# Attention and two feed-forward layers on one core: TensorE's order written out from pair seven on, with transposes as two 64-row products

## The chip, the core and the metric

The kernel runs on one core of one Trainium2 chip. The metric is the device time of one execution in microseconds, the median of three runs. The core's engines are TensorE (PE in the profile, its weight loads PEld), VectorE (DVE), ScalarE (ACT), GpSimd (POOL) and SyncE (SP), which issues nearly all DMAs.

## The reference

There are 4 batches of 8 heads, 576 positions and a head size of 64. The attention's output, as 2304 tokens of 512 features, goes through two feed-forward layers, of inner size 1536 and 2048.

```
    scores = scale * np.matmul(q, k.transpose(0, 1, 3, 2))
    log_f = np.log(np.clip(f, 0.0001, 1.0))
    cum = np.cumsum(log_f, axis=-1)
    decay = cum[:, :, :, None] - cum[:, :, None, :]
    ...
    scores = np.where(causal, -1000000000.0, scores + decay)
    scores = scores - np.max(scores, axis=-1, keepdims=True)
    attn = np.exp(scores)
    attn = attn / (np.sum(attn, axis=-1, keepdims=True) + 1e-09)
    return np.matmul(attn, v).astype(np.float32)
...
    gate = 1.0 / (1.0 + np.exp(-(x @ w_gate)))
    val = x @ w_val
    return (gate * val @ w_out).astype(np.float32)
...
    h = x @ w_in
    relu6 = np.clip(h + 3.0, 0.0, 6.0)
    g = h * relu6 / 6.0
    return (g @ w_out).astype(np.float32)
```

## The kernel before, in words

**Attention** works on 16 pairs of heads, four per batch. A pair has four units, which are blocks of 128 query rows (s = 1, 2, 3, of which s = 1 holds the first two blocks) and the tail of 64 rows of both heads (s = 4). Pairs 0 to 6 take them upwards, pairs 7 to 15 downwards (4, 3, 2, 1). One unit passes through these stages:

- `scores`: products `st<-kp,qp`, one per head, each on 64 of the array's rows, or `st<-kp,qz` on all 128 rows for the tail. Each writes its own one of three PSUM banks (`psA`).
- `expo`: VectorE adds the decay and takes the row minimum (L443), ScalarE exponentiates (L451). `norm`: VectorE takes the reciprocal (L485, L486), GpSimd multiplies (L488).
- `flip`: TensorE transposes the 128x128 blocks of `e` with an identity into `tt` or `t5` (three banks, `psB`), ScalarE copies them to `etA` (s = 1) or `etB` (L525). A pair has 25 such blocks: 5, 8, 6 and 6 for s = 4, 3, 2, 1. `etA` and `etB` exist once each, so a pair's first copy into `etB` waits until the pair before has read it.
- `values`: `pv<-etB,vn` and `pv<-etA,vn`, on 64 columns of the array for each head. ScalarE and VectorE split the result into two parts (`x`, L550, L551), and `store` sends them to DRAM (`x_d`, L555).

The loop over t does `scores` of unit t, `norm` of t - 1, `flip` of t - 2 and `values` of the pair whose last unit was t - 3.

**Feed-forward groups as filler.** While attention runs, TensorE also works on the first layer for chunks of 512 tokens, in groups of 12 products of 128x512: `pg<-big,wg` (gate), `pv<-big,wv` (value), `po<-big,wo` (down). A group's four feature blocks are read back from `x_d` into `big` (L205), one block for each head pair of a batch, so the last block of a chunk is there only after the batch's last pair is stored. Chunk 1 needs pair 7, chunk 2 pair 11. The groups' PSUM tiles come from `psF` (two banks). `Filler.step` hands out groups at a pace.

**What sets the order.** The program is recorded and a scheduler orders each engine's instructions, by priority and by its own estimate of the times. `tc.keep_in_program_order` (through `pe.rows` and `pe.once`) pins an instruction behind those pinned before it. Before the change, flips are pinned, and a first product of the values; scores and groups are placed by the scheduler, also in the middle of one another.

After attention the rest of the first layer and the whole second layer follow, on TensorE almost alone.

Of the kernel before, what the change touches and what calls it, by code (L numbers as in the profile page):

```python
# [7 lines left out]
F32 = mybir.dt.float32  # L8
# [4 lines left out]
ALU = mybir.AluOpType  # L13
# [7 lines left out]
def attn_moe_kernel(  # L21
# [232 lines left out]
    reads, banks = [], []  # L254

    def row(first, *a, **k):

        with ExitStack() if first else tc.high_priority():
            mm = pe.matmul(*a, **k)
        if not first and not pe.rows:  # L260
            tc.keep_in_program_order(mm)
        return mm

    def after_read(mm, n):

        if n >= 0:
            tc.add_manual_dep(
                mm.ins, reads[n].ins.name,
                mybir.DependencyInfo(mybir.DependencyClass.Sync, mybir.DependencyReason.DATA), reason="both banks",
            )  # L270

# [30 lines left out]
    class Pair:  # L302
# [56 lines left out]
        def prep(self):  # L359


            sc = -1.0 / 8.0
            qp = self.qp = qk2.tile([P, NQ * P], F32, tag="qp", name="qp")
            kp = self.kp = qk2.tile([P, S], F32, tag="kp", name="kp")
            qz_ = self.qz = qz[self.i % 2]
            if self.blocks:
                nc.vector.transpose(qp, self.qn[:, : NQ * P])
                nc.vector.transpose(kp, self.kn)
                for j in range(2):
                    r = slice(64 * j, 64 * j + 64)  # L370
                    nc.vector.transpose(qz_[r, r], self.qn[r, NQ * P :])
                return
            tq = psB.tile([P, 512], F32, tag="B", name="tq")
            for c in range(NQ):
                pe.transpose(tq[:, c * P : (c + 1) * P], self.qn[:, c].rearrange("p h d -> p (h d)"), ident)
            nc.vector.tensor_scalar(qp, tq, sc, 1.0, ALU.mult, ALU.mult)
            tk = psB.tile([P, 512], F32, tag="B", name="tk")
            for c in range(NQ):
                pe.transpose(tk[:, c * P : (c + 1) * P], self.kn[:, c].rearrange("p h d -> p (h d)"), ident)
            if self.i < KD:  # L380
                nc.vector.tensor_copy(kp[:, : NQ * P], tk)
            else:
                nc.scalar.copy(kp[:, : NQ * P], tk)
            tl = psB.tile([P, 512], F32, tag="B", name="tl")
            pe.transpose(tl[:, :P], self.kn[:, NQ].rearrange("p h d -> p (h d)"), ident)
            nc.scalar.copy(kp[:, NQ * P :], tl[:, :TAIL])
            for j in range(2):
                r = slice(64 * j, 64 * j + 64)
                nc.vector.tensor_scalar(qz_[r, r], tl[r, TAIL:P], sc, 1.0, ALU.mult, ALU.mult)
# [14 lines left out]
        def scores(self, s):  # L404
# [3 lines left out]
            self.both = banks[len(banks) + 1 - NA] if len(banks) + 1 >= NA else -1  # L408
# [26 lines left out]
            for c, st in enumerate(self.sts):  # L435
                pe.matmul(st[:, :hs], self.qz, self.kp[:, c * hs : (c + 1) * hs], start=True, stop=True)
# [52 lines left out]

        def flip(self, s):  # L490
# [5 lines left out]
            if s == next(x for x in self.order if x >= 2):  # L496

                self.etB = et.tile([P, 2, NQ, 320], F32, tag="etB", name="etB")
            jobs = []
            if s == 1:  # L500
                for j in range(2):
                    tt = psB.tile([P, 512], F32, tag="B", name="tt")
# [4 lines left out]
                    jobs.append((self.etA[:, j], tt[:, : 3 * P]))  # L507
            elif s < NQ:
                for j in range(2):
                    tt = psB.tile([P, 512], F32, tag="B", name="tt")  # L510
# [3 lines left out]
                    jobs.append((dst, tt[:, : (s + 1) * P].rearrange("p (a b) -> p a b", b=P)))  # L514
            else:
                e = es[0]
                tt = psB.tile([P, 512], F32, tag="B", name="tt")
                for kt in range(NQ):
                    pe.transpose(tt[:, kt * P : (kt + 1) * P], e[:, kt * P : (kt + 1) * P], ident)
                t5 = psB.tile([P, 512], F32, tag="B", name="t5")  # L520
                pe.transpose(t5[:, :P], e[:, S - P :], ident)
                jobs.append((self.etB[:, :, :, 256:320], tt.rearrange("p (a j b) -> p j a b", j=2, b=TAIL)))
                jobs.append((self.etB[:, :, NQ - 1, 0:TAIL], t5[:, :P].rearrange("p (j b) -> p j b", j=2)))
            for dst, src in jobs:
                nc.scalar.copy(dst, src)  # L525
            del self.es[s], self.m[s]

        def values(self, part, behind=False):
# [5 lines left out]
            pool, tag = (psF, "F") if FV(self) else (psB, "B")  # L534
            o = pool.tile([P, 512], F32, tag=tag, name="pv")[:, :n]
# [15 lines left out]
            nc.vector.tensor_tensor(xl, o, xh.bitcast(F32), ALU.subtract)  # L551
# [95 lines left out]
    class Filler:  # L647
# [17 lines left out]
        def run(self):  # L665
# [16 lines left out]
            yield from last.down()  # L682

# [449 lines left out]
    FV = lambda p: p.i < 5  # L1133
# [5 lines left out]
    KD, TL, KT = 4, 3, 7  # L1139
# [40 lines left out]
    def scores(t):  # L1180
# [5 lines left out]
        if i == 0 and nxt:  # L1186
            with behind(decay if p.i == 0 else None):
                nxt.load()
                nxt.load_decay()
                nxt.load_v()  # L1190
        p.scores(s)
# [37 lines left out]

    def some(t):  # L1230
# [86 lines left out]
```

## Time and profile before

| what | us |
|---|---|
| median of 3 runs | 1016.67 (1016.11 to 1018.33) |
| the profiled execution, its own time | 1017.3 |
| span of that execution, first to last instruction | 1015.5 |
| TensorE busy | 1000.9 (99%) |
| VectorE, ScalarE, GpSimd busy | 535.1, 460.1, 305.5 |

The profiled execution's 1017.3 us is its span of 1015.5 us and 1.8 us around it. In the rows, "x12" is a count of instructions in a merged stretch; a product in plain float32 (scores, values) counts as two instructions, a transpose or a product of the groups as one. The time behind the start of a stretch lasts until its last instruction ends, and so overlaps the next stretch, which has begun by then; the step from one start to the next is what TensorE spent. "<-" names what the engine waited for.

### The profile page before, as it was taken

How to read it: one execution, taken by the hardware profiler on the slowest of the kernel's cores; microseconds unless marked ns; L12 is line 12 of the kernel's file. 1: busy time of each engine (PE TensorE's matmuls, PEld its weight loads, DVE VectorE, ACT ScalarE, POOL GpSimd, SP SyncE). 2: the span in 40 equal slices, each digit the busy share in tenths (PEclk: the TensorE clock that was granted, in tenths of full speed). 3: DMA queues.
4: the chain of work that ended last, by engine and by line, in shares of the span. 5: the costliest groups of instructions: out<-in, count | busy, mean ns of one | idle time of the engine just before them, and what ended most of it. 6: DMA issues, size and time to landing. Idle time of an engine off the chain costs nothing.

```text
span 1015.5 us, 15368 instructions
## 1 busy us (share of the span) xinstructions
PE 1000.9 (99%) x5329; PEld 823.7 (81%) x5329; DVE 535.1 (53%) x1216; ACT 460.1 (45%) x1034; POOL 305.5 (30%) x385
## 2 busy tenths in 40 slices
PE   7999999999999999999999999999999999999998
PEld 4666666667678889988888888898998998989987
DVE  5788854655516644648668565544535444333222
ACT  5786565565534532424334334443434433333332
POOL 3678745546414221210424222111111111111110
PEclk9999999999999999999999999999999999999999
DMA  7998677463233344366777477756594845754211
GB/s 197 261 270 228 177 213 194 106 214 116 89 127 125 124 125 147 127 230 254 270 287 290 151 280 275 272 180 226 192 365 168 299 171 192 290 196 155 77 71 63
DMA packets 141214, 197.84 MB, mean 195 GB/s; under 512 B 84208, under 2 KB 93424, under 8 KB 137040
## 3 DMA queue, kind: packets, MB, share of 16 engines
q1 hardware_dynamic: 141040, 196.71, 58.2%
q8 instruction: 42, 0.69, 0.3%
q14 instruction: 36, 0.29, 0.1%
q10 hardware_dynamic: 96, 0.15, 0.1%
HBM read 143.47 MB, written 53.36 MB: 194 GB/s over the span
## 4 chain that ended last, share of the span: by engine, by line
PE 88%; DVE 4%; POOL 2%; DMA 2%; ACT 2%; issue 1%; SPq 1%; POOLq 0%; DVEq 0%; ACTq 0%
PE po L216 34%; PE pv L216 17%; PE u L216 17%; PE pg L216 13%; PE st L216 4%; PE tt L220 3%; POOL e L488 1%; ACT e L451 1%; DVE e L443 1%; DMA big<-x_d 1%; SPq L333 1%; POOL dt L354 1%; DMA dc<-cum_d 0%; DMA raw<-in_moe_w_val_dram 0%; DVE big L65 0%
## 5 line engine op out<-in xcount | busy, mean ns | idle before, releaser
L216 PE MATMUL po<-w,big 128*128 128x512 f32 x864 | 200.5, 390 | 0.0
L216 PEld LDWEIGHTS po<-w,big 128*128 128x128 f32 x864 | 161.8, 188 | 32.8
L216 PE MATMUL pg<-big,wg 128*128 128x512 f32 (+1 forms) x720 | 163.7, 371 | 1.2 <-DMA big<-x_d 1.0
L216 PE MATMUL po<-big,wo 128*128 128x512 f32 (+1 forms) x720 | 163.3, 372 | 1.1 <-POOL wo L64 1.1
L216 PE MATMUL pv<-big,wv 128*128 128x512 f32 (+1 forms) x720 | 164.2, 372 | 0.0
L216 PEld LDWEIGHTS po<-big,wo 128*128 128x128 f32 x720 | 124.9, 189 | 26.0 <-issue 2.2
L216 PEld LDWEIGHTS pg<-big,wg 128*128 128x128 f32 x720 | 125.4, 189 | 24.6 <-DMA big<-x_d 1.2
L216 PEld LDWEIGHTS pv<-big,wv 128*128 128x128 f32 x720 | 125.1, 189 | 24.6 <-issue 2.6
L1059 DVE TENSOR_TENSOR h<-h,u 128x384 f32<-128x384 f32 x69 | 38.2, 554 | 154.7 <-PE u L216 154.7
L451 ACT ACTIVATE e<-e,m 128x256 f32<-128x256 f32 (+4 forms) x144 | 83.9, 584 | 54.8 <-DVE m L443 49.5
L488 POOL TENSOR_SCALAR e<-e,m 128x256 f32<-128x256 f32 (+4 forms) x144 | 87.3, 621 | 59.1 <-DVE m L486 28.4
L216 PE MATMUL u<-h,big 128*128 128x384 f32 x504 | 90.5, 336 | 0.5 <-DVE h L1059 0.4
L216 PE MATMUL u<-h,h 128*128 128x384 f32 x504 | 90.1, 336 | 0.0
L216 PEld LDWEIGHTS u<-h,big 128*128 128x128 f32 x504 | 88.2, 188 | 2.1 <-DVE h L1059 1.1
L1008 POOL TENSOR_TENSOR big<-tail,big 128x384 fp32r<-128x384 f32 x30 | 30.6, 1018 | 196.5 <-PE u L216 116.1
L216 PEld LDWEIGHTS u<-h,h 128*128 128x128 f32 x504 | 88.4, 188 | 1.0
L1056 ACT COPY h<-u 128x384 f32<-128x384 f32 x69 | 32.8, 475 | 111.7 <-PE u L216 111.7
L771 DVE SCALAR_TENSOR_TENSOR sg<-sg,pv 128x512 f32<-128x512 f32 (+1 forms) x48 | 29.7, 618 | 91.4 <-PE pv L216 62.0
L111 ACT ACTIVATE raw<-raw 128x512 f32<-128x512 f32 x68 | 45.5, 681 | 64.7 <-DVE raw L108 59.4
L443 DVE CUSTOM_DVE_ANT_0 e<-st,dc 128x384 f32<-128x384 f32 (+3 forms) x110 | 53.8, 519 | 33.7 <-PE st L216 21.2
L114 DVE SCALAR_TENSOR_TENSOR raw<-raw 128x512 int32<-128x512 int32 x68 | 54.4, 810 | 17.1 <-ACT raw L111 16.7
L220 PE MATMUL tt<-ident,e 128*128 128x128 f32 x384 | 55.4, 276 | 2.6 <-POOL e L488 1.2
(139 smaller groups left out, 1218.5 us busy)
## 6 DMA issues: line engine op xcount, KB each, us to landing
h<-xc_d SPq DMA_DIRECT2D x21, 768.0 KB, 7.1
big<-x_d SPq DMA_DIRECT2D x28, 512.0 KB, 5.2
raw<-in_moe_w_out_dram SPq DMA_DIRECT2D x28, 512.0 KB, 3.7
h<-wt_d SPq DMA_DIRECT2D x12, 1024.0 KB, 7.3
big<-wt_d SPq DMA_DIRECT2D x12, 1024.0 KB, 7.3
dc<-cum_d SPq DMA_DIRECT2D x16, 576.0 KB, 5.4
x_d<-x SPq DMA_DIRECT2D x16, 576.0 KB, 3.4
h<-wb_d SPq DMA_DIRECT2D x12, 768.0 KB, 4.5
```

Of the source, the lines that this page charges most:

```text
L111: nc.scalar.activation(e, e, AF.Copy, scale=2.0**-112)
L114: nc.vector.scalar_tensor_tensor(low, high, 3, low, ALU.logical_shift_left, ALU.bitwise_or)
L216: i = nc.tensor.matmul(*a, **k)
L220: i = nc.tensor.transpose(*a)
L333: nc.sync.dma_start(t[32 * g : 32 * g + 32].rearrange("r (t c) -> r t c", c=32), src[self.b, 2 * self.hp + g // 2, :, g % 2 * 32 : g % 2 * ...
L443: i = nc.vector.tensor_tensor_reduce(out=e, in0=st, in1=d, op0=ALU.add, op1=ALU.min, scale=self.by, scalar=init, accum_out=m[:, a : a + 1],)
L451: nc.scalar.activation(e, e, AF.Exp, bias=m[:, a : a + 1], scale=-1.0, accum_out=m[:, 4 + b : 5 + b])
L488: nc.gpsimd.tensor_scalar(e, e, m[:, 12 + j : 13 + j], 1.0, ALU.mult, ALU.mult)
L771: pace["dve"] = nc.vector.scalar_tensor_tensor(sg, sg, 1.0, pv, ALU.add, ALU.mult)
L1008: (nc.vector if f else nc.gpsimd).tensor_tensor(lo, sg, hi.bitcast(F32), ALU.subtract)
L1056: nc.scalar.copy({0: u1, 2: u2, 3: p5}[s], o)
L1059: tt(c, c, o, ALU.add)
```

## The change

From pair seven (`RT` = 7, t from 28) the stages of a step are recorded as `fixed`, `expo`, `norm`, `prep`, and everything that `fixed` puts on TensorE is pinned: the scores of unit t, the transposes of unit t - 2, and then either the values of the finished pair or one whole filler group. In these pairs a 128x128 block is transposed as two products, each with 64 of the block's rows as weights and a 64x64 identity as the moving part; the two halves of all blocks go to two banks, and ScalarE's copies are laid out by half. The first transpose of a flip waits until both banks are free, and the first score product of the tail waits for both of its banks, as those of other units do. The values of pairs from 6 on go to `psF`.

```diff
+    def bank(name):
+        users.append([])
+        return psB.tile([P, 512], F32, tag="B", name=name), users[-1]
...
+        def flip_rows(self, s, es):
+            halves, free = [], []
+            for h in range(2):
+                tt, used = bank("tt")
+                halves.append((tt, used))
+                free += users[-4]
...
+            for a, e in enumerate(blocks):
+                for h in (1, 0):
+                    tt, r, first = halves[h][0], slice(64 * h, 64 * h + 64), a == 0 and h == 1
+                    mm = row(first, tt[:, 64 * a : 64 * a + 64], e[r], ident[r, r], flip=True)
+                    if first:
+                        depend(mm, free)
...
+                else:
+                    jobs.append((self.etB[:, h, :, 256:320], tt[:, :256].rearrange("p (a b) -> p a b", b=64), used))
+                    jobs.append((self.etB[:, h, NQ - 1, 0:TAIL], tt[:, 256:320], used))
+            for dst, src, by in jobs:
+                by.append(nc.scalar.copy(dst, src))
...
+        def one(self):
+            got = next(self.groups, None) if self.groups else None
+            self.out += bool(got)
+            return got
...
-    FV = lambda p: p.i < 5
+    FV = lambda p: p.i < 5 or p.i >= RT - 1
...
+    def fixed(t):
+        scores(t)
+        pe.rows = True
+        p, s = unit(t - 2)
+        if p:
+            p.flip(s)
+        p, s = unit(t - 3)
+        if p and s == p.order[-1]:
+            values(t)
+        elif t < len(units) + 2:
+            fill.one()
+        pe.rows = False
...
-        for job in (scores, values, expo, flip, norm, some, prep):
+        for job in (fixed, expo, norm, prep) if t >= NQ * RT else (scores, values, expo, flip, norm, some, prep):
             job(t)
```

The order shows the change at three places. The first, on TensorE, is where pair seven's first transposes and the first down group meet, before:

```order
L216 MATMUL po<-big,wo_1720 128x512
L216 MATMUL st<-kp,qp 128x128 x2
L216 MATMUL st<-kp,qp 128x256 x2
L216 MATMUL pv<-etB,vn_151 64x64 x2
L216 MATMUL pv<-etA,vn_151 64x256 x2
L216 MATMUL pv<-etA,vn_151 64x128 x2
L220 MATMUL tt<-ident,e 128x128 x4
L216 MATMUL po<-big,wo_1720 128x512 x2
L216 MATMUL st<-kp,qz_144 128x288
L216 MATMUL po<-big,wo_1720 128x512 x2
L216 MATMUL po<-big,wo_1550 128x512 x4
L216 MATMUL st<-kp,qz_144 128x288
```

The same place of the change (`vn_151` holds pair six's values, `wo_1550` and `wo_1720` are the two tiles of down weights that a group needs, six products with each):

```order
L216 MATMUL st<-kp,qp 128x384 x2
L220 MATMUL tt<-ident,e 128x64 x10
L216 MATMUL pv<-etB,vn_151 64x320 x6
L216 MATMUL pv<-etB,vn_151 64x192 x2
L216 MATMUL pv<-etB,vn_151 64x64 x2
L216 MATMUL pv<-etA,vn_151 64x256 x2
L216 MATMUL pv<-etA,vn_151 64x128 x2
L216 MATMUL st<-kp,qp 128x128 x2
L216 MATMUL st<-kp,qp 128x256 x2
L220 MATMUL tt<-ident,e 128x64 x16
L216 MATMUL po<-big,wo_1550 128x512 x6
L216 MATMUL po<-big,wo_1720 128x512 x6
```

Before, the scheduler splits the down group: three products with `wo_1720` stand ahead of the tail's scores, and the rest behind. Now the group stands in one piece, its six products with `wo_1720` together.

The second place on TensorE is where pair seven's values end and chunk 1's first gate group begins, before (`wg_746` are gate weights):

```order
L216 MATMUL pv<-etA,vn_152 64x256
L216 MATMUL pv<-etA,vn_152 64x128 x2
L220 MATMUL tt<-ident,e 128x128 x4
L220 MATMUL t_2008<-ident,e 128x128
L216 MATMUL st<-kp,qz_145 128x288
L216 MATMUL st<-kp,qp 128x512 x2
L220 MATMUL tt<-ident,e 128x128 x14
L216 MATMUL st<-kp,qp 128x384 x2
L220 MATMUL tt<-ident,e 128x128 x6
L216 MATMUL pg<-big,wg_746 128x512 x15
L216 MATMUL pv<-etB,vn_153 64x320 x6
```

And in the change:

```order
L216 MATMUL pv<-etA,vn_152 64x256 x2
L216 MATMUL pv<-etA,vn_152 64x128 x2
L216 MATMUL st<-kp,qp 128x128 x2
L216 MATMUL st<-kp,qp 128x256 x2
L220 MATMUL tt<-ident,e 128x64 x16
L216 MATMUL po<-big,wo_1550 128x512 x6
L216 MATMUL po<-big,wo_1720 128x512 x6
L216 MATMUL st<-kp,qz_145 128x288 x2
L220 MATMUL tt<-ident,e 128x64 x12
L216 MATMUL pg<-big,wg_746 128x512 x12
```

Before, nine products of the first gate group and six of the second stand together, and their last three, which read the last feature block, come after the next values. Now the first group's twelve products stand in one piece, two steps behind the pair that writes its last block.

The third place is ScalarE's, around a pair's values (`sg` and `xs` belong to groups, `raw` to weights), before:

```order
L451 ACTIVATE e,m<-e,m 128x384 x2
L111 ACTIVATE raw<-raw 128x512
L550 CAST x<-pv 128x320
L550 CAST x<-pv 128x256
L525 COPY etB<-tt 128x8x64
```

And in the change:

```order
L470 ACTIVATE e,m<-e,m 128x384 x2
L541 COPY etB<-tt 128x4x64
L541 COPY etB<-tt 128x64
L541 COPY etB<-tt 128x4x64
L541 COPY etB<-tt 128x64
L606 CAST x<-pv 128x320
L606 CAST x<-pv 128x256
```

The tail's transposes now stand ahead of the values on TensorE, and so their copies, four in place of two, stand ahead of the values' casts on ScalarE.

## Rows read from the trace of the kernel before

**Rows 1.** The page: busy time and share of the span by engine.
```profile
PE 1000.9 (99%) x5329; PEld 823.7 (81%) x5329; DVE 535.1 (53%) x1216; ACT 460.1 (45%) x1034; POOL 305.5 (30%) x385
```

**Rows 2.** TensorE's waits, 119.5 to 292 us: total, times, longest.
```profile
PE po L216 <- POOL wo L64: 1.1, 1, 1.1
PE pg L216 <- DMA big<-x_d: 1.0, 1, 1.0
PE st L216 <- DVE m L443: 0.6, 2, 0.3
PE tt L220 <- POOL e L488: 0.4, 1, 0.4
```

**Rows 3.** TensorE's waits, 292 to 1015 us.
```profile
PE u L216 <- DVE h L1059: 0.4, 1, 0.4
```

**Rows 4.** Timeline of TensorE: start, length, instruction; transposes and values.
```profile
187.47 1.03 PE L220 MATMUL tt<-ident,e 128*128 128x128 f32 x8
188.34 0.65 PE L216 MATMUL st<-kp,qz 128*128 128x288 f32 x2
...
198.52 2.27 PE L216 MATMUL pv<-etB,vn 128*64 128x320 f32 x20
200.63 0.82 PE L216 MATMUL pv<-etA,vn 128*64 128x256 f32 x8
```

**Rows 5.** Timeline of the weight loads, from 204.04 to 204.16 us.
```profile
204.04 0.29 PEld L216 LDWEIGHTS st<-kp,qp 64*128 64x128 f32 x3 [0.36 <-issue]
```

**Rows 6.** All weight loads of scores: duration min/median/max.
```profile
L216 PEld LDWEIGHTS st<-kp,qp x256: 182/186/330, 7.9 to 276.2; 64*128 64x128 f32 x128
```

**Rows 7.** All weight loads of transposes.
```profile
L220 PEld LDWEIGHTS tt<-ident,e x384: 137/140/144, 18.1 to 288.4; 128*128 128x128 f32 x192
```

**Rows 8.** Timeline of the weight loads, from 201.37 to 201.44 us.
```profile
201.38 0.20 PEld L220 LDWEIGHTS tt<-ident,e 128*128 128x128 f32 x2 [0.17 <-issue]
```

**Rows 9.** Timeline of TensorE: a group among groups.
```profile
316.66 2.88 PE L216 MATMUL po<-big,wo 128*128 128x512 f32 x12
```

**Rows 10.** Timeline of TensorE: a group between scores on 64 and on 128 rows.
```profile
238.03 0.93 PE L216 MATMUL st<-kp,qp 64*128 64x128 f32 x8
238.89 3.02 PE L216 MATMUL pv<-big,wv 128*128 128x512 f32 x12
241.75 0.65 PE L216 MATMUL st<-kp,qz 128*128 128x288 f32 x2
```

**Rows 11.** Timeline of TensorE where pair seven's third unit is scored.
```profile
119.48 0.92 PE L216 MATMUL st<-kp,qp 64*128 64x384 f32 x4
120.32 1.65 PE L216 MATMUL po<-big,wo 128*128 128x512 f32 x6
```

**Rows 12.** Timeline of GpSimd at the down weights.
```profile
128.30 0.65 POOL L64 TENSOR_SCALAR wo<-raw 128x512 fp32r<-128x512 f32 x1
129.03 1.32 POOL L65 TENSOR_TENSOR wo<-raw,wo 128x512 fp32r<-128x512 f32 x1
```

**Rows 13.** SyncE's DMA issues behind pair eleven's values.
```profile
222.31 0.37 SPq L555 DMA_DIRECT2D x_d<-x  x1
...
226.16 0.37 SPq L205 DMA_DIRECT2D big<-x_d  x1
```

**Rows 14.** Timeline of TensorE, the same stretch.
```profile
219.91 0.82 PE L216 MATMUL pv<-etA,vn 128*64 128x256 f32 x8
...
227.39 3.45 PE L216 MATMUL pg<-big,wg 128*128 128x512 f32 x14
```

**Rows 15.** The page: DMA issues, KB each and median us to landing.
```profile
big<-x_d SPq DMA_DIRECT2D x28, 512.0 KB, 5.2
```

**Rows 16.** ScalarE's copy of one full bank of transposes.
```profile
221.41 0.59 ACT L525 COPY etB<-tt 128x512 f32<-128x512 f32 x1 [0.23 <-PE tt L220]
```

**Rows 17.** One unit's scores and its last step, on TensorE and GpSimd.
```profile
212.09 1.13 PE L216 MATMUL st<-kp,qp 64*128 64x512 f32 x4
...
218.26 1.37 POOL L488 TENSOR_SCALAR e<-e,m 128x512 f32<-128x512 f32 x2
```

More of the change, by code (lines that the diff above doesn't have):

```diff
@@ L251, in attn_moe_kernel, with row @@
         nc.gpsimd.memset(t[:TAIL, NQ], 0.0)
-    reads, banks = [], []
-    def row(first, *a, **k):
+    reads, banks, users = [], [], []
+    def row(first, *a, flip=False, **k):
         with ExitStack() if first else tc.high_priority():
-            mm = pe.matmul(*a, **k)
+            mm = pe.transpose(*a) if flip else pe.matmul(*a, **k)
         if not first and not pe.rows:
@@ L270, in after_read, with depend, free_banks @@
             )
+    def bank(name):
+        users.append([])
+        return psB.tile([P, 512], F32, tag="B", name=name), users[-1]
+    def depend(mm, on):
+        for i in on:
+            tc.add_manual_dep(
+                mm.ins, i.ins.name,
+                mybir.DependencyInfo(mybir.DependencyClass.Sync, mybir.DependencyReason.DATA), reason="both banks",
+            )
+    def free_banks():
+        return banks[len(banks) + 1 - NA] if len(banks) + 1 >= NA else -1
     def cumulate():
@@ L406, in scores @@
             self.sts = [psA.tile([P, 512], F32, tag="A", name="st") for j in range(2)]
-            self.both = banks[len(banks) + 1 - NA] if len(banks) + 1 >= NA else -1
+            self.both = free_banks()
             if s < NQ:
@@ L435, in scores @@
             for c, st in enumerate(self.sts):
-                pe.matmul(st[:, :hs], self.qz, self.kp[:, c * hs : (c + 1) * hs], start=True, stop=True)
+                mm = row(c == 0, st[:, :hs], self.qz, self.kp[:, c * hs : (c + 1) * hs], start=True, stop=True)
+                if c == 0 and self.i >= RT:
+                    after_read(mm, self.both)
         def expo(self, s):
@@ L488, in norm @@
                 nc.gpsimd.tensor_scalar(e, e, m[:, 12 + j : 13 + j], 1.0, ALU.mult, ALU.mult)
+        def flip_rows(self, s, es):
[4 more added lines that the diff above has]
+                free += users[-4]
+            if s == 1:
+                blocks = [es[x + y][:, c : c + P] for x in (0, 2) for y, c in ((0, 0), (1, 0), (1, P))]
+            elif s < NQ:
+                blocks = [e[:, kt * P : (kt + 1) * P] for e in es for kt in range(s + 1)]
+            else:
+                blocks = [es[0][:, c : c + P] for c in (0, P, 2 * P, 3 * P, S - P)]
+            for a, e in enumerate(blocks):
[4 more added lines that the diff above has]
+                        depend(mm, free)
+            jobs = []
+            for h, (tt, used) in enumerate(halves):
+                if s == 1:
+                    dst = self.etA.rearrange("p j (a h b) -> p j a h b", a=3, h=2)[:, :, :, h]
+                    jobs.append((dst, tt[:, : 6 * 64].rearrange("p (j a b) -> p j a b", j=2, a=3), used))
+                elif s < NQ:
+                    c = (s - 2) * P + 64 * h
+                    dst = self.etB[:, :, 0 : s + 1, c : c + 64]
+                    jobs.append((dst, tt[:, : 2 * (s + 1) * 64].rearrange("p (j a b) -> p j a b", j=2, b=64), used))
+                else:
+                    jobs.append((self.etB[:, h, :, 256:320], tt[:, :256].rearrange("p (a b) -> p a b", b=64), used))
+                    jobs.append((self.etB[:, h, NQ - 1, 0:TAIL], tt[:, 256:320], used))
+            for dst, src, by in jobs:
+                by.append(nc.scalar.copy(dst, src))
+            del self.es[s], self.m[s]
         def flip(self, s):
@@ L501, in flip @@
                 for j in range(2):
-                    tt = psB.tile([P, 512], F32, tag="B", name="tt")
+                    tt, used = bank("tt")
                     pe.transpose(tt[:, :P], es[2 * j], ident)
@@ L1137, in attn_moe_kernel @@
     WU = 24
-    KD, TL, KT = 4, 3, 7
+    KD, TL, KT, RT = 4, 3, 7, 7
     CA, C0, CB, CC = 0.65, 8, (1.8, 1.0, 1.5, 1.7, 2.0), 1.0
@@ L1190, in scores @@
                 nxt.load_v()
+        pe.rows = t >= NQ * RT
         p.scores(s)
```

42 lines of the change are left out of this document (22 added, 20 removed).

## The prediction

> **What bounds the kernel now.** I read the page first: TensorE is busy for 99% of the span and no other engine for much over half [rows 1]. Any time saved on TensorE therefore shows in the end, unless it turns into a wait there. Its waits come next. Between 119.5 us, where pair seven's third unit is scored, and 292 us, where the last pair's values end, it waited five times, 3.1 us in all: for down weights from GpSimd, for a feature block from DRAM, twice for VectorE, once for a normalised block [rows 2]. Behind 292 us there is only one wait of 0.4 us that the trace names [rows 3]; what attention gives up earlier, the rest of the program passes on. So the sum is made on TensorE alone, over the stretch from pair seven to the end of attention, in three kinds of terms: what transposes cost, what switching the array's shape costs, and waits.
>
> **Transposes, removed and added.** Nine pairs (7 to 15) have 25 blocks each, 225 in all. Before, eight in a row take from 187.47 to 188.34 us [rows 4], 0.109 us a block, 24.5 us together. The change makes two products of 64 rows and 64 columns of each block. No such transpose is in the trace, so I bound it from both sides. Two products that each take half the array do run side by side: the ten pairs of instructions of a values product, 2,432 columns for each head, go from 198.52 to 200.63 us [rows 4], 0.87 ns a column for the two together. By the moving columns alone a block then costs 64 x 0.87 = 0.055 us. But each half also loads 128 columns of weights, and the load may last longer. For scores on 64 rows, a stretch of three loads lasts 0.29 us [rows 5] and one load 0.186 us [rows 6], so the third started 0.104 us behind the first two: that is the upper end, 0.104 us a block and almost nothing gained. Loads of transposes are shorter, 0.140 against 0.186 us [rows 7, 6], and when one starts a run, the next follows after 0.20 - 0.14 = 0.06 us [rows 8]. The new products are transposes, so I am nearest to that row and take 0.06 us: 225 x (0.109 - 0.060) = 11.0 us saved, between 1.1 us (0.104) and 12.2 us (0.055). The two halves go to two banks, as the two heads' scores do, so I see no new conflict there.
>
> The trace shows the load of 128 columns taking 0.104 us for scores and 0.06 us for transposes [rows 5, 8]. The Trainium skill ("TensorE: Matmul & The Clock Gate", section LDWEIGHTS) says that a load's time goes by its columns, divided by 1.2 GHz, and not by its rows. By that figure, an estimate, each half would cost 107 ns as a whole block did, and the saving would be 225 x 0.002 = 0.5 us. The row of the scores agrees with it and that of the transposes does not; it is one of the rivals below.
>
> **Switching shape.** Going from 128 rows to 64 rows or to 64 columns and back costs something: twelve products among groups last 2.88 us [rows 9], but 3.02 us behind scores on 64 rows [rows 10], so 0.14 us a switch. Counted in the two orders from pair seven's second unit to the last values there are 71 switches before and 76 in the change (the new transposes sit beside scores or values of half shape, but also between the tail's scores and a group, which were of one shape). Five more cost 0.7 us.
>
> **Waits that go.** All five waits of [rows 2] belong to an order that no longer stands; I count 3.1 us as gone and put new ones in.
>
> **Waits that come.** Groups are now whole and pinned, so what a group lacks stops TensorE, and with it the next unit's scores.
>
> First place: the first down group. The third unit's scores start at 119.48 us and take 0.84 us [rows 11]; then ten half transposes (0.3), pair six's values (198.52 to 200.63 + 0.82 us [rows 4], 2.9), the next scores (0.86, [rows 10]), sixteen halves (0.5), nine products of the group (2.1) and three switches (0.4): TensorE reaches the second half of the second weight tile at about 127.4 us. GpSimd has its high part at 128.30 + 0.65 = 128.95 us and its low part at 129.03 + 1.32 = 130.35 us [rows 12]; the first two of the three products need the high part, the third the low one. So it waits 1.6 us, works 0.5 us, waits 0.9 us: 2.5 us. GpSimd's order there is the same in both programs, so I leave its times.
>
> Second place, twice: the first gate group of chunks 1 and 2. Its tenth product needs the block that the last pair has just stored. For pair eleven the values end at 219.91 + 0.82 = 220.73 us, the tenth product of the next gate group runs near 227.39 + 9 x 0.23 = 229.5 us without a wait [rows 14], so the block was there within 8.8 us. In the change the tail's copies stand ahead of the casts; they move 640 columns, at 0.59 us for 512 [rows 16] some 0.8 us, so the block comes after 9.6 us. TensorE wants it after scores (0.9), sixteen halves (0.5), a down group (2.7), the tail's scores (two of 0.65 us [rows 10] that overlap, 1.1), twelve halves (0.4), nine products (2.1) and four switches (0.6): 8.3 us, hence a wait of 1.3 us. If the read takes the page's median of 5.2 us to land [rows 15], rather than the 3.3 us that 229.5 allows behind its issue at 226.16 us [rows 13], it is 1.9 us more, 3.2 us. SyncE's queue also holds the next pair's loads between store and read. I take 2.0 us each, 4.0 us for both, nearer to the block that was seen to land.
>
> Elsewhere: a flip now follows its scores by a fixed way. From the start of a 512-column score (1.13 us, [rows 17]) it is twelve halves, a group, scores, ten halves, values, scores, four switches: 1.1 + 0.4 + 2.7 + 0.8 + 0.3 + 2.9 + 0.9 + 0.6 = 9.7 us. In the trace the same unit's last multiplication ends at 218.26 + 1.37 = 219.63 us, 7.5 us behind the start at 212.09 us [rows 17], with ScalarE and VectorE half idle [rows 1]. 2.2 us are left, so these waits are nothing in the middle case; what covers them is the group and the values between. Two more copies a pair on ScalarE are hidden by the same idle half. I put 1.0 us for small misses over nine pairs, an allowance that I chose; its bounds are 0 and the rival below.
>
> **Sum.** -11.0 + 0.7 - 3.1 + 2.5 + 4.0 + 1.0 = -5.9 us. The profiled execution's 1017.3 us (span 1015.5 us and 1.8 us around it) would become 1011.4 us; it lies 0.6 us above the median of 1016.67 us, so the median would become 1010.8 us, 0.6% faster.
>
> **Rivals.** *The halves don't pay.* If each half's load takes what the scores' load takes, 0.104 us a block, the saving shrinks to 1.1 us and the rest stands: -1.1 + 5.1 = +4.0 us, 1020.7 us. By the rule of the Trainium skill's page on TensorE in place of that row (0.5 us saved) the whole would be 1021.3 us. For it speaks [rows 5], against it [rows 8]. It decides where a block costs more than 0.109 - 5.1 / 225 = 0.086 us. Chance 12%.
>
> *The pinned order starves TensorE.* The way from scores to normalised block becomes longer than 9.7 us, because VectorE, ScalarE and GpSimd still take them in the scheduler's order among weights and groups. Each two steps then last as long as that way, and a pair has four steps. At 10.5 us, 3.0 us over the 7.5 us seen, a pair grows by 2 x 0.8 = 1.6 us, nine pairs by 14.4 us: 1025 us. It turns the gain over from 10.0 us on, where 18 x 0.33 = 5.9 us are gone. For it: GpSimd waited for ScalarE and VectorE in its turn, and one wait on a block is in [rows 2]. Against it: 2.2 us of room. Chance 13%.
>
> *The round trip is slow.* If each chunk's block comes 5 us late, three more than I took, the two waits are 10 us and the sum is +0.1 us: 1016.8 us, no change. The wait that stood in chunk 1 before, although its products had been put last [rows 2], speaks for it; pair eleven's block speaks against it. Chance 15%.
>
> *Nothing waits anew.* The weights come in time and the chunks too, and a block costs 0.055 us: -12.2 + 0.7 - 3.1 = -14.6 us, 1002.1 us. Chance 5%.
>
> That the halves aren't made, or not in pairs, is excluded: the order shows 450 of them from pair seven on.
>
> **How the numbers follow.** The forecast has the remaining 55%, with 1010.8 us and its own range from 1005 us (no wait at chunks and no small misses: 5 us less) to 1015 us (3.2 us at each chunk, and 2 us more of small misses). The range of 1004 to 1020 us adds the slow round trip and the near ends of its neighbours, and leaves out the halves at their full price, deep starvation and the best case. A measurement of this kernel tells about 0.2%, 2 us, from no change. Faster by more: the forecast's part below 1014.6 us, 53%, the best case, 5%, and 5% of the slow round trip's milder end, 63%. Slower: the two rivals' 25%, less 3% at their mild ends, 22%. The rest, 15%, is within.
>
> **What would show it.** In the changed profile: transposes in pairs that step by 0.06 us; their sum in that stretch down by some 11 us; TensorE waiting near 128 us for `wo` and behind pairs seven and eleven for `big`; no long list of waits for the normalised `e`; and values of the last pair ending near 286 us rather than 292 us. The prediction is wrong if halves step by 0.1 us, or if waits of TensorE in that stretch sum to well over 7.5 us.

## The result, and the profile after

The changed kernel takes 1024.78 us (median of four, 1024.53 to 1025.69) against 1017.04 us for the kernel before on the same chip (1016.11 to 1018.33): a ratio of 1.0077, 95% interval 1.0059 to 1.0094. It is slower by 0.8%, where 0.6% faster was forecast. The profiled execution took 1024.54 us, its span is 1022.8 us.

TensorE's row of the page, against [rows 1]:

```profile
PE 998.4 (98%) x5554; PEld 823.3 (80%) x5554; DVE 535.9 (52%) x1216; ACT 457.6 (45%) x1052; POOL 303.5 (30%) x385
```

TensorE is busy for 2.5 us less than before, and the span is 7.3 us longer. So its idle time grew by 9.8 us. Its waits from 115 to 300 us answer to [rows 2]:

```profile
PE pg L216 <- DMA big<-x_d: 5.3, 2, 3.3
PE tt L220 <- POOL e L507: 5.1, 2, 4.1
PE po L216 <- DVE x L607: 0.5, 1, 0.5
PE pv L216 <- DVE x L607: 0.4, 2, 0.2
PE pv L216 <- DVE sg L687: 0.3, 1, 0.3
```

They are 11.6 us, where 3.1 us stood before and 7.5 us were forecast. Of the old waits, those for `wo` and for `m` are gone; those for `big` and for `e` are longer than before. Behind 292 us there is still only one wait of 0.4 us for `h`, as in [rows 3], so what attention loses is lost in the end.

But waits are not all of it. The windows of the changed kernel give stretch, its length, the engines' busy time, and then the granted clock of TensorE (after the last parenthesis):

```profile
0.00:20.00 20.00, 14.55 (x63) 7.11 (x64) 9.54 (x32) 7.05 (x17) 6.52 (x21) 0.91 0.77 192
120.00:140.00 20.00, 15.53 (x106) 10.99 (x106) 13.98 (x38) 9.51 (x30) 14.61 (x21) 0.83 0.65 186
...
160.00:180.00 20.00, 17.30 (x113) 11.70 (x113) 8.48 (x30) 9.64 (x29) 7.97 (x13) 0.83 0.36 90
```

In the kernel before, each of these three stretches has 1.00. The timeline of TensorE shows where the clock was lost in the two later stretches, at the two longest waits:

```profile
131.98 1.12 PE L220 MATMUL tt<-ident,e 64*128 64x64 f32 x16 [4.13 <-POOL e L507]
133.18 5.18 PE L216 MATMUL po<-big,wo 128*128 128x512 f32 x12
138.20 1.14 PE L216 MATMUL st<-kp,qz 128*128 128x288 f32 x4
...
139.79 3.00 PE L216 MATMUL po<-big,wo 128*128 128x512 f32 x12
...
162.50 1.65 PE L216 MATMUL pg<-big,wg 128*128 128x512 f32 x3 [3.26 <-DMA big<-x_d]
164.08 2.08 PE L216 MATMUL st<-kp,qp 64*128 64x512 f32 x4
165.95 0.85 PE L220 MATMUL tt<-ident,e 64*128 64x64 f32 x12
166.74 3.87 PE L216 MATMUL pg<-big,wg 128*128 128x512 f32 x12
170.54 0.92 PE L216 MATMUL st<-kp,qp 64*128 64x384 f32 x4
...
238.18 0.96 PE L216 MATMUL pg<-big,wg 128*128 128x512 f32 x3 [2.07 <-DMA big<-x_d]
...
240.50 3.03 PE L216 MATMUL pg<-big,wg 128*128 128x512 f32 x12
243.46 0.92 PE L216 MATMUL st<-kp,qp 64*128 64x384 f32 x4
```

The same instructions stand behind the waits of chunks 1 and 2: three products, scores, twelve halves, a group, and then the next scores. Behind 2.07 us of waiting they take 243.46 - 238.18 = 5.28 us, behind 3.26 us they take 170.54 - 162.50 = 8.04 us: 2.8 us more. The products, the scores and the halves take nearly twice their time there, at the lower of the clock's two levels (1.2 in place of 2.4 GHz), and the clock is back within the group behind them. At pair seven the group steps by 138.20 - 133.18 = 5.02 us where the next one, at 139.79, steps by 2.92 (scores follow at 142.71), and the sixteen halves step by 1.20 us, against 0.59 us for the next pair's: 2.7 us more. So some 5.5 us went behind waits, on top of them.

What stood in the way at pair seven is not the normalised block that the row names: GpSimd had ended that `e` at 126.69 us, over 5 us earlier (its timeline):

```profile
125.08 1.61 POOL L507 TENSOR_SCALAR e<-e,m 128x512 f32<-128x512 f32 x2 [1.02 <-DVE m L505]
```

The first transpose waits until both of its banks are free, and one of the two still had to be read by the copies of the tail's transposes. ScalarE's timeline:

```profile
130.86 0.65 ACT L111 ACTIVATE raw<-raw 128x512 f32<-128x512 f32 x1 [2.98 <-DVE m L504]
131.42 0.85 ACT L541 COPY etB<-tt 128x256 f32<-128x256 f32 x4
```

The copies stand behind `raw`, a step of the weight conversion, for which ScalarE stands idle 2.98 us. `raw` waits for VectorE, and VectorE's timeline shows what it did in that time:

```profile
126.94 0.68 DVE L107 TENSOR_SCALAR raw<-raw 128x512 int32<-128x512 int32 x1
128.11 1.77 DVE L65 TENSOR_TENSOR big<-sg,big 128x512 fp32r<-128x512 f32 x1 [0.49 <-POOL big L64]
129.80 0.88 DVE L108 SCALAR_TENSOR_TENSOR raw<-raw 128x512 int32<-128x512 int32 x1
```

VectorE's half of a group's result (`big`, itself waiting for GpSimd) stands between two steps of `raw`. It takes 1.77 us here, where the same instruction takes 0.69 us at 100.37 us; GpSimd works on `wo` beside it (L65, 128.05 to 129.33 us). The kernel before has the same slow instruction (1.78 us at 123.67 us), so it is not what the change brought.

### The profile page after: what moved, and what is told of

It is laid out like the page before. It is cut to its first block, busy times and chain, and to the rows that moved or that the text cites. A ratio compares the mean times of both kernels' runs of the same rounds, so it can differ in the third digit from the quotient of the medians.

```text
span 1022.8 us, 15796 instructions
## 1 busy us (share of the span) xinstructions
PE 998.4 (98%) x5554; PEld 823.3 (80%) x5554; DVE 535.9 (52%) x1216; ACT 457.6 (45%) x1052; POOL 303.5 (30%) x385
## 4 chain that ended last, share of the span: by engine, by line
PE 88%; DMA 3%; DVE 3%; POOL 2%; ACT 2%; issue 1%; SPq 0%; POOLq 0%; DVEq 0%; ACTq 0%
PE po L216 33%; PE pv L216 17%; PE u L216 17%; PE pg L216 14%; PE st L216 4%; PE tt L220 2%; DMA big<-x_d 2%; POOL e L507 1%; DMA x_d<-x 1%; DVE e L462 1%; ACT etB L541 1%; DMA dc<-cum_d 0%; DVE x L607 0%; POOL dt L371 0%; DVE raw L108 0%
## 5 line engine op out<-in xcount | busy, mean ns | idle before, releaser
L216 PE MATMUL pv<-big,wv 128*128 128x512 f32 (+1 forms) x720 | 161.1, 370 | 0.4 <-DVE x L607 0.4
L216 PEld LDWEIGHTS po<-big,wo 128*128 128x128 f32 x720 | 127.2, 191 | 24.0 <-DVE x L607 0.9
L507 POOL TENSOR_SCALAR e<-e,m 128x256 f32<-128x256 f32 (+4 forms) x144 | 84.5, 601 | 73.0 <-DVE m L505 36.6
L220 PEld LDWEIGHTS tt<-ident,e 64*128 64x128 f32 (+1 forms) x618 | 38.3, 143 | 23.8 <-issue 10.9
```

What stands on the lines that cost most here:

```text
L216: i = nc.tensor.matmul(*a, **k)
L220: i = nc.tensor.transpose(*a)
L507: nc.gpsimd.tensor_scalar(e, e, m[:, 12 + j : 13 + j], 1.0, ALU.mult, ALU.mult)
```

## The experiments

All ratios are to the kernel before on the same chip. The first four kernels shared a median of 1018.08 us for it, the next four 1018.30, then three 1018.01, and the last had 1017.30 us. Where two kernels ran on different chips, their ratios are compared and not their times. Runs without a diff combine edits that are shown elsewhere in this section.

**The halves alone**: the loop and the placement of the kernel before, the values' old banks, `flip_rows` kept.

```diff
-    FV = lambda p: p.i < 5 or p.i >= RT - 1
+    FV = lambda p: p.i < 5
-        pe.rows = t >= NQ * RT
-        for job in (fixed, expo, norm, prep) if t >= NQ * RT else (scores, values, expo, flip, norm, some, prep):
+        for job in (scores, values, expo, flip, norm, some, prep):
```

> The transposes are made in halves from pair seven on, but the hand-written order is left out: scores, flips, values and groups go back to the scheduler's placement, and the values to their bank of before. Theory A (the halves pay, and what costs is that the pinned order waits in three places, with half clock behind two of them): about 1011 us (1008 to 1014), the halves' saving of 7 to 10 us less 1.4 us for the tail's scores, whose changed recording also moves instructions ahead of pair seven. Theory B (the halves cost more than they save, by switches of shape): 1017 us or above. Theory C (the pinned order is too tight for the other engines everywhere): as A here.

Measured: 1028.08 us, ratio 1.0101 (1.0070 to 1.0132). The time lies in theory B's range, but the trace does not show theory B's reason, switches of shape. A and C, which foresaw 1011 us, failed. What the trace does show is waits for banks; TensorE's waits from 100 to 300 us begin with this row:

```profile
PE tt L220 <- ACT etB L541: 7.8, 7, 1.7
```

A flip of halves needs two of the three banks of `psB` at once. The kernel before filled them one after the other.

**The order alone**: whole blocks in the pinned order.

```diff
-            if self.i >= RT:
-                return self.flip_rows(s, es)
```

> The hand-written order stays, and the transposes are whole blocks again. A: the saving of the halves is lost, some 7 to 10 us above the change: 1032 to 1035 us. B: no slower than the change, 1017 to 1025 us. C: about as A, since longer steps leave more room, 1025 to 1032 us.

Measured: 1026.73 us, ratio 1.0084 (1.0067 to 1.0100), against 1.0077 (1.0059 to 1.0094) for the change: no difference that these runs can tell. So in this order the halves gain next to nothing. The time lies in theory C's range; but the waits stand in the change's three places, not everywhere. They come with the order: 5.3 us for `big`, and 3.71 us at pair seven, where the row names the copy of the bank:

```profile
129.90 1.09 PE L220 MATMUL tt<-ident,e 128*128 128x128 f32 x4 [3.71 <-ACT etB L579]
130.83 5.32 PE L216 MATMUL po<-big,wo 128*128 128x512 f32 x12
...
236.51 0.97 PE L216 MATMUL pg<-big,wg 128*128 128x512 f32 x3 [2.51 <-DMA big<-x_d]
...
238.66 1.54 PE L220 MATMUL tt<-ident,e 128*128 128x128 f32 x6
239.86 3.84 PE L216 MATMUL pg<-big,wg 128*128 128x512 f32 x12
```

The half clock is there too, with whole blocks: at pair seven and behind chunk 2's wait of 2.51 us. Behind chunk 1's longer wait of 2.78 us the clock stays full.

**The groups a step later**: no group at t = 31.

```diff
-        elif t < len(units) + 2:
+        elif NQ * RT + 3 != t < len(units) + 2:
```

> The change, but the step of pair seven's last scores (t = 31) gets no group, so that every later group comes one step later and each chunk's first gate group stands some 4 us further behind the values that feed it. A: the two waits for the feature block (3.3 and 2.1 us) and the half clock behind the first (2.8 us) go, 1017 us (1015 to 1019); the wait of 4.1 us at pair seven's first long flip stays. B: 1024 us. C: at best 2 us less, 1023 us, because the waits reappear at other flips.

Measured: 1018.33 us, ratio 1.0005 (0.9996 to 1.0014): theory A. The change's loss is gone, although the wait at pair seven stays (4.2 us). The waits for `big` fall to 0.5 us, and the clock is 1.00 from 160 to 180 us.

**The tail's second product as before in pairs 0 to 6.** The change gives it a pinned place in all pairs.

```diff
-                mm = row(c == 0, st[:, :hs], self.qz, self.kp[:, c * hs : (c + 1) * hs], start=True, stop=True)
+                mul = pe.matmul if self.i < RT else lambda *a, **k: row(c == 0, *a, **k)
+                mm = mul(st[:, :hs], self.qz, self.kp[:, c * hs : (c + 1) * hs], start=True, stop=True)
```

> The change, but the tail's second score product is recorded as before in pairs 0 to 6, so that TensorE's order ahead of pair seven is that of before, row for row. A: 1.4 us less than the change, 1023.4 us, with no wait of 1.0 us for a feature block near 85 us. B and C: 1024.8 us, since nothing that they blame is touched.

Measured: 1022.0 us, ratio 1.0038 (1.0017 to 1.0058), its executions from 1017.49 to 1027.16 us. That is 0.4% below the change's ratio, where theory A foresaw 0.14% and B and C nothing; with such a spread the edit's own share can't be told. The wait near 85 us falls from 1.03 to 0.47 us. The profiled execution, at 1019.39 us, shows one thing that the spread can come from. It waits as long at chunk 1, and keeps the full clock behind it:

```profile
159.41 0.97 PE L216 MATMUL pg<-big,wg 128*128 128x512 f32 x3 [3.32 <-DMA big<-x_d]
160.31 1.13 PE L216 MATMUL st<-kp,qp 64*128 64x512 f32 x4
...
161.73 3.03 PE L216 MATMUL pg<-big,wg 128*128 128x512 f32 x12
164.69 0.92 PE L216 MATMUL st<-kp,qp 64*128 64x384 f32 x4
```

5.28 us again, with 3.32 us of waiting ahead. A wait of this length may cost its own length, as here, or 2.8 us more, as in the change.

**`raw` on VectorE around pair seven.**

```diff
-            conv.run(CS if len(conv.jobs) <= 2 * NSA - 6 * NGA else CE if t < 16 else CA, EA)
+            conv.run(CS if len(conv.jobs) <= 2 * NSA - 6 * NGA else CE if t < 16 else CA, (nc.vector, *EA[1:]) if 26 <= t < 32 else EA)
```

> The changed kernel, but around pair seven (t from 26 to 31) the one step of the weight conversion that stood on ScalarE (`raw`, L111) is done by VectorE, which does the steps before and behind it. Theory A: TensorE's 4.13 us in front of pair seven's sixteen halves, which the profile puts down to GpSimd's `e`, are a wait for a PSUM bank, and the bank's copies stood on ScalarE behind `raw`, which stood idle for 2.98 us for VectorE. Then the wait shrinks below 1.5 us, the down group behind it takes 3.0 us in place of 5.18, and the time is 1018 to 1021 us. Rival B: the wait is for the normalised block, as the profile names it; then it stays at 4 us and the time at 1024 to 1026 us. Rival C: VectorE's queue is itself the delay, and the step only moves it: about 2 us of the wait stay, 1022 to 1023 us.

Measured: 1022.7 us, ratio 1.0044 (1.0026 to 1.0062), the time of rival C. The sixteen halves no longer wait, so ScalarE was what held them. But the wait only moves, to the group behind them, whose bank VectorE has yet to read:

```profile
126.07 0.68 PE L220 MATMUL tt<-ident,e 64*128 64x64 f32 x16
129.93 4.60 PE L216 MATMUL po<-big,wo 128*128 128x512 f32 x12 [3.19 <-DVE x L607]
```

What is late at pair seven is VectorE's queue.

The same trace has half clock behind a shorter wait, at pair eleven:

```profile
207.43 0.71 PE L220 MATMUL tt<-ident,e 64*128 64x64 f32 x16 [1.54 <-POOL e L507]
208.63 4.58 PE L216 MATMUL po<-big,wo 128*128 128x512 f32 x12 [0.49 <-DVE x L607]
```

The group takes 1.6 us more than the 3.0 us of others.

**TensorE kept busy in the waits for `big`.**

```diff
+                    for _ in range((0, 20, 13)[self.c] if i == 0 else 0):
+                        pe.matmul(pg[:, : 3 * P], identb, masks, start=True, stop=True)
                     up(pg, self.wg, i, self.xk, KC if self.c < 1 else 0 if i == 0 else KC)
```

> The changed kernel, with 20 and 13 products of 128x384 in bfloat16 (0.162 us each at the start of the program) that write into the tile of chunk 1's and chunk 2's first gate group ahead of it and are overwritten; they do 3.24 and 2.1 us of work that nothing needs, about as much as TensorE waits for `big` there (3.26 and 2.07 us). Theory A: the half clock behind chunk 1's wait belongs to the idle time. Then the waits shrink to under 0.5 us, the three products, the scores and the next gate group behind them take 0.96, 1.13 and 3.04 us again in place of 1.65, 2.08 and 3.87, and the time falls by 2 to 3 us, to 1022 to 1023 us, although TensorE does more. Rival B: the half clock has nothing to do with the idle time; then the groups stay slow, or the time doesn't move: 1024 to 1026 us.

Measured: 1020.85 us, ratio 1.0016 (1.0003 to 1.0029). TensorE does 5.3 us more work, and the ratio falls from 1.0077 to 1.0016. The stretch behind chunk 1's wait is back at full clock, 165.89 - 160.64 = 5.25 us; 1.23 us of the wait were left, since the block came later:

```profile
153.90 3.42 PE L216 MATMUL pg<-masks,identb 128*128 128x384 bf16 x20
...
160.64 0.96 PE L216 MATMUL pg<-big,wg 128*128 128x512 f32 x3 [1.23 <-DMA big<-x_d]
...
162.96 3.00 PE L216 MATMUL pg<-big,wg 128*128 128x512 f32 x12
```

One execution would not show it, since a wait can pass without half clock. But the mean clock of all ten executions is 0.994 to 0.998, and that of the change's four is 0.990 to 0.993. So chunk 1's half clock belongs to the idle time, as theory A said. The fall of the time is more than it explains: between pair seven's 512-column scores and the last values the profiled execution gains 1.5 us, and 3.1 us lie ahead of them, where the clock of the first 20 us was 1.00.

**The three edits together** (a step later, the tail's product as before, `raw` on VectorE).

> The changed kernel with three edits together: no group at t = 31, so that all later ones come a step later; the tail's second product placed as before in pairs 0 to 6; `raw` on VectorE around pair seven. Theory A: the parts add up. From the 1018.3 us of the shift alone, 1.4 us for the tail's products ahead of pair seven, 3 us of the wait that is left at pair seven and some 2.2 us of half clock behind it go: 1010 to 1013 us, faster than the kernel before by 0.5 to 0.8%. Rival B: each wait removed shows another behind it, since the pinned order leaves too little room; then 1016 to 1019 us, as the shift alone.

Measured: 1017.65 us, ratio 0.9996 (0.9985 to 1.0006): rival B. A wait of 3.9 us is left at pair seven, now in front of the tail's scores, for VectorE's `m`, and the clock is 0.83 from 120 to 140 us. Taking the group away at t = 31 also took away work that could cover that queue; that this is why the wait stays was not tried.

**The same with whole blocks.** It prices the halves.

> The same three edits, with whole blocks of 128 rows transposed in place of the halves. It prices the halves where little else waits. Theory A: a pair takes 17.1 us with halves and 18.05 with whole blocks between pair starts that nothing disturbs, 0.9 us, over nine pairs 8 us: 1018 to 1021 us, 7 to 9 us above the kernel with the halves. Rival B: the time between them is the 2 us that the changed kernel and the one with whole blocks differed by; then under 4 us.

Measured: 1020.07 us, ratio 1.0015 (1.0004 to 1.0025), 2.4 us above the halves: rival B, for the whole. In this part of pair fourteen nothing waits in either kernel. With halves:

```profile
242.64 0.54 PE L220 MATMUL tt<-ident,e 64*128 64x64 f32 x12
243.11 3.01 PE L216 MATMUL pg<-big,wg 128*128 128x512 f32 x12
246.05 0.92 PE L216 MATMUL st<-kp,qp 64*128 64x384 f32 x4
246.80 0.47 PE L220 MATMUL tt<-ident,e 64*128 64x64 f32 x10
247.20 2.27 PE L216 MATMUL pv<-etB,vn 128*64 128x320 f32 x20
```

With whole blocks:

```profile
247.10 0.88 PE L220 MATMUL tt<-ident,e 128*128 128x128 f32 x6
247.73 3.01 PE L216 MATMUL pg<-big,wg 128*128 128x512 f32 x12
250.67 0.92 PE L216 MATMUL st<-kp,qp 64*128 64x384 f32 x4
251.52 0.66 PE L220 MATMUL tt<-ident,e 128*128 128x128 f32 x4
252.01 0.27 PE L220 MATMUL t<-ident,e 128*128 128x128 f32 x1
252.21 2.27 PE L216 MATMUL pv<-etB,vn 128*64 128x320 f32 x20
```

Six blocks step by 0.47 and 0.63 us, the scores behind them by 0.75 and 0.85, five blocks by 0.40 and 0.69 us. From one pair's 512-column scores to the next it is 17.13 us with halves (136.91 to 154.04) and 18.05 with whole blocks (227.99 to 246.04) where nothing waits, 0.92 us a pair. But with halves four of the seven steps from pair eight on take 17.30 to 18.49 us: short waits, mostly for a bank of `psF`, take a part of it back. The seven steps together are 122.07 us with halves and 127.31 with whole blocks, 0.75 us a pair.

**The pinned order from pair eight**, the tail's product as before ahead of it (that edit is the one shown above), no group at t = 33.

```diff
-    KD, TL, KT, RT = 4, 3, 7, 7
+    KD, TL, KT, RT = 4, 3, 7, 8
-        elif t < len(units) + 2:
+        elif NQ * RT + 1 != t < len(units) + 2:
```

> The pinned order and the halves begin with pair eight (`RT` = 8) in place of seven, the tail's second product stands as before in the pairs ahead, and no group stands at t = 33, so that chunk 1's and chunk 2's first gate groups come a step later. `raw` stays on ScalarE. Theory A: the 3.9 us that TensorE still waited at pair seven with three edits, and the half clock behind it (some 2 us), belong to the place where the pinned order starts while VectorE and GpSimd still convert the down weights; the scheduler's own order passes that place with little waiting. Against 1017.65 us there: less 3.9, less 1 to 2, and 0.9 more for pair seven's whole blocks: 1011 to 1014 us, faster than the kernel before by 0.4 to 0.7%. Rival B: the place moves with the start: a wait of 3 to 4 us stands at pair eight, 1016 to 1019 us.

Measured: 1013.62 us, ratio 0.9950 (0.9934 to 0.9967), as theory A said: faster than both kernels. TensorE's waits from 80 to 300 us are ten, none over 0.9 us, 5.3 us in all, and at pair seven, where the scheduler's own order now stands, the clock stays at 1.00:

```profile
120.00:140.00 20.00, 18.64 (x109) 11.95 (x109) 14.32 (x41) 11.39 (x31) 12.82 (x20) 1.00 0.51 164
```

**The same without the step's shift.**

> The same without the step's shift: chunk 1's and chunk 2's first gate groups stand two steps behind the pair that stores their last block, as in the changed kernel. It prices these two waits alone, against the kernel with the shift. Theory A: 3.3 and 2.1 us of waits for `big`, less the 0.5 us that the shift leaves, and half clock behind the longer one in part of the executions (0 to 2.7 us): 5 to 8 us above the kernel with the shift. Rival B: it is hidden, since the shift moves one group of 2.9 us behind attention: under 2 us apart.

Measured: 1021.3 us, ratio 1.0025 (1.0010 to 1.0039): 7.7 us above, within theory A's 5 to 8. The waits for `big` are 5.2 us, the longer 3.7 us, with half clock behind it. The gate groups' place is worth more than all that the halves save (the last run).

**The halves in the scheduler's order, with the values in `psF`.**

```diff
-    FV = lambda p: p.i < 5
+    FV = lambda p: p.i < 5 or p.i >= RT - 1
```

(The diff is to the kernel with the halves alone.)

> The halves in the scheduler's own order, as in the run of the halves alone, but the values of pairs from 6 on go to `psF`, as in the changed kernel. Theory A: the halves alone lost their gain since a flip needs two of the three banks at once, which the values of these pairs used too; with the values elsewhere TensorE's waits for ScalarE's copies of `etB` fall from 7.8 to under 3 us, and the time from 1028 to 1019 to 1023 us. Rival B: two banks of three for each flip are the limit, with or without values: the waits for `etB` stay at 6 us or more, 1026 to 1030 us.

Measured: 1022.91 us, ratio 1.0039 (1.0023 to 1.0054). The time is that of theory A, the waits for `etB` at 5.2 us lie between the two: the values had a share in the banks' shortage, and the larger part of these waits stays with two banks of three for each flip.

**The fastest kernel with whole blocks.**

> The fastest kernel so far (pinned order from pair eight, the step's shift), with whole blocks of 128 rows transposed in place of the halves: the price of the halves where TensorE waits least. Theory A: eight pairs at the 0.92 us by which an undisturbed pair differed (18.05 against 17.13 us) are 7.4 us: 1020 to 1022 us on a chip where the kernel with the halves takes 1013.6 us. Rival B: a part of it fills waits that whole blocks don't have, as the 2.4 us between the medians of the two kernels with three edits say: 1015 to 1018 us.

Measured: 1016.96 us, ratio 0.9998 (0.9989 to 1.0007). By the two ratios the halves are worth 0.48%, 4.9 us, less than theory A's 7.4 and just more than rival B allows. With whole blocks this pinned order takes the time of the kernel before. In pair eleven the halves wait for `e` (0.33 us) and the group behind them for a bank (0.48 us), and the pair takes 18.51 us, against 18.43 with whole blocks: there the time won was already idle.

## Why the prediction was wrong

**What bounds the kernel** stood: TensorE, and nothing behind attention gives the loss back.

**Transposes and switching**, -11.0 + 0.7 = -10.3 us. Right in mechanism, since two halves do run side by side, but somewhat too large. Five and eight blocks of halves step by 0.40 and 0.59 us (147.85 to 148.25; 151.87 to 152.46 in the changed kernel), so three blocks more take 0.19 us, 0.063 us each, where 0.060 was taken from [rows 8]. That it came so near is partly luck: [rows 8] are two whole blocks at the start of a run, and in a run such blocks step by 0.109 us, so the row is no price of halves. Over a whole pair, switches included, halves save 0.92 us against whole blocks in the same pinned order, where the prediction had 10.3 / 9 = 1.14 against the scheduler's order: -8.3 us over nine pairs.

The Trainium skill ("TensorE: Matmul & The Clock Gate", section LDWEIGHTS) prices a load by its columns alone, by which a block in two halves is estimated at 0.107 us; the measured 0.063 us differs, and decides. The Trainium skill ("TensorEngine Tiling (Array Packing)", section Key Properties) says that different tiles can load weights and multiply in parallel; the 0.063 us agrees with that.

**Waits that go**, -3.1 us: right as a count, though one of them did not go. Chunk 1's wait for `big` stands in front of the same three products, grown from 1.0 to 3.3 us; it is counted anew below.

**Waits that come, first place**, +2.5 us: the place was right, the cause wrong, and the size 4.1 us. The step counted the down weights and took GpSimd's order as all that could be late. The flip's own demand, both banks free at once, with ScalarE's copies behind `raw` and VectorE's queue behind both, came first, and the wait for `wo` lay hidden behind it. GpSimd's times, which the step left as they were, moved too: the two parts of [rows 12] end at 133.37 and 134.75 us, 4.4 us later. The group begins at 133.18 us and needs them for its last products; without the flip's wait it would have begun near 128.4 us (estimated from 126.92 us, with 0.9 us for the scores and 0.6 us for the halves) and waited for `wo`. In the kernel that starts at pair eight, which has the scheduler's order at this place, that wait is 0.7 + 0.7 us.

**Second place**, +4.0 us: 3.3 and 2.1 us, 5.3 us. Right as waits, at the upper bound of 3.2 us for chunk 1 and at the chosen 2.0 us for chunk 2. The next pair's loads did stand between SyncE's store at 152.72 us and its read of `big` at 156.18 us.

**Small misses**, +1.0 us: 2.2 us (1.0 for a block, the rest for banks of `psF`). No long list of waits for `e` came, so the rival of a starved TensorE is refuted. The sign of being wrong that the prediction named, waits well over 7.5 us, came: 11.6 us.

**The step that failed** is in "Waits that come": each wait was counted at its own length. Behind the two longest ones TensorE runs at half clock, 5.5 us that the sum hasn't got, the largest of its misses. The wait, not the change's work, brings it. For chunk 1 this is shown with TensorE kept busy; at pair seven it is there with whole blocks too, and gone where no long wait stands (from pair eight). It does not come behind each wait, and the length alone does not decide it: waits of 2.78 and 3.32 us passed without it, and in the run with the groups a step later it stands behind 0.88 and 0.66 us shortly after one another (near 280 us), where the same two, 0.88 and 0.65 us, pass without it in the kernel with three edits. The Trainium skill ("TensorE: Matmul & The Clock Gate", section HAM oscillation — how this bites in real kernels) tells of matmuls that run at the lower clock behind waits for a DMA; the changed kernel's trace agrees at 3.26 us, and the two waits of 2.78 and 3.32 us, both for a DMA, show that it need not come.

**A part of the change was not priced**: the tail's second product, which the change pins for all pairs, not from pair seven on. Pair seven's 512-column scores, before and after:

```profile
114.14 1.13 PE L216 MATMUL st<-kp,qp 64*128 64x512 f32 x4
```

```profile
117.92 1.13 PE L216 MATMUL st<-kp,qp 64*128 64x512 f32 x4
```

Of these 3.8 us, some 2.5 are the start of the program: two kernels here that are the same up to this place (from pair eight, with and without the shift) reach it at 116.44 and 113.95 us, with a clock of 0.91 and 1.00 in the first 20 us, and the profiled execution of the change had 0.91. That part is chance, not the change: three of the fourteen profiled executions have 0.91, one of them of the fastest kernel. The rest, some 1.3 us, may be the pinned product. With the first 20 us at 1.00, four kernels that have it and keep the pinned order reach this place at 114.83 to 115.86 us; the kernel before and four that haven't do so at 113.95 to 115.06 us. The two overlap, so its price is about 1 us and not firmly shown.

**The sum again.** From that place to the end of the last values it was 177.9 us before (to 292.07 us) and is 180.3 us (to 298.26 us), with five products of groups fewer, worth 1.2 us: +3.6 us for the same work. The terms as measured, -8.3 - 3.1 + 4.1 + 5.3 + 2.2 + 5.5, give +5.7 us; 2 us of difference have no owner here. The 0.92 us a pair is against whole blocks in the pinned order, so what that order itself gains or loses in switches is among them. With 3.8 us ahead it is +7.4 us, the 7.3 us of the spans.

Not settled: which waits bring the half clock, and why VectorE and GpSimd fall behind at pair seven by just these 4 us; what is shown is only that a start at pair eight avoids it.

## What to carry to other kernels

Pinning an engine's order makes each of its waits real: before pinning, list for every pinned group what it needs, banks to write into among them, and put the group that needs a round trip through DRAM one step later than seems enough. Here that one step was worth more than the arithmetic that was saved.

A wait of TensorE should be priced with what may run at half clock behind it: here 2.8 us behind 3.26 us, 2.7 us behind 4.13 us, 1.6 us behind 1.54 and 0.49 us, and nothing behind 2.07, 2.78 and 3.32 us. The length of the wait does not tell which it will be, so one kernel's executions can differ by it.

A faster form of a product that needs two buffers at once, where one did, is priced with the buffers: the halves alone made this kernel slower by 1%, and in an order that suits them they are worth 0.5%.

## What the runs showed of the hardware

Two transposes on 64 rows each, side by side, cost 0.063 us a block of 128x128, against 0.109 us for the block in one. A wait of 3.26 us was followed by 8.04 us for work that takes 5.28 us; one of 3.32 us, with the same instructions behind it, by 5.28 us. And 33 products that nobody needs, 5.3 us of work put into two waits, did not lengthen the program: a ratio of 1.0016 to the kernel before with them, 1.0077 without.
